# A new table of operations for an attention and MLP kernel: what stands where in each engine's queue

## The chip, the cores and the metric

The kernel runs on one core of a Trainium2 chip. The metric is device time in microseconds (us) of one execution; the time of a version is the median of several runs. A profile shows one execution, instruction by instruction, on the engines TensorE (PE, with its weight loads as PEld), VectorE (DVE), ScalarE (ACT), GpSimd (POOL) and the queue of SyncE that issues DMAs (SP).

## The reference

For 2048 tokens of width 512 the kernel computes an attention layer, gated by an MLP, and a residual:

```python
def _A_ref(x, wqkv, wo):                     # 32 heads of 16, window of 8 keys, 2 apart
    qkv = (x @ wqkv).reshape(B, S, 3, H, Dh) ...
    idx = pos[:, None] - (jnp.arange(8) * 2)[None, :]
    logits = einsum("bhsd,bhswd->bhsw", q, k[idx]) * scale      # idx < 0: -1e9
    o = einsum("bhsw,bhswd->bhsd", softmax(logits), v[idx])
    return o.reshape(B, S, D) @ wo
def _B_ref(x, w1, b1, w2, b2):
    return gelu(layernorm(x) @ w1 + b1) @ w2 + b2               # 512 -> 1376 -> 512
xn = layernorm(A_x)
return A_x + _A_ref(xn, ...) * silu(_B_ref(xn, ...))
```

## The kernel before

The tokens are split into two halves by parity (c = 0, 1), since the window goes in steps of 2, and each half into 8 tiles of 128 tokens. Every matrix is held as a high and a low half of 16 bits, and a product is three matmuls (high-high, high-low, low-high), summed in PSUM.

The work is a list of 1262 operations, each with one engine, a few instructions, and the data that it reads and writes:

- Loading and normalising the tokens, L659 to L773: statistics, y = (x - mean) / deviation on ACT (L744), DVE (L751) or POOL (L748), a transpose on PE (L766) and the split of the result (L770, L773). Two tiles are projected directly in 32-bit floats (L700).
- Projections q, k, v (PE, L864; 12 matmuls of 384 columns for a tile and a quarter of the heads), brought out of PSUM by ACT (L882) or DVE (L878) into a buffer U.
- Eight units of attention, one for each half and quarter of the heads, nearly all on DVE: products of q and shifted keys (L930), their sums (L933), softmax (L953 to L962), products with the values (L988, in the last unit L1026) and their sums (L983; on POOL L998 and L1008). The result is split into halves (ACT L971, DVE L973) and transposed by a DMA (L976).
- The MLP: first layer on PE (L1141), gelu and high half on ACT (L1154, L1157), low half on DVE (L1159), second layer on PE (L1184, with a last narrow block at L1172 and L1175), silu on ACT (L1195, L1200).
- The output layer: for the first half of the tokens L1054 on PE, the gate on DVE (L1068), the residual (L1045) and the store (L1048); for the second half L1086, L1118, the residual on DVE (L1125) or POOL (L1122), and the stores (L1127). In the second half the matmuls of three quarters of the heads come first and those of the last quarter, whose transposed attention is the last to come, later into the same PSUM tile. The last tile is computed and stored in two parts of 256 columns.
- 24 filler matmuls without a use (L1303).

What sets the order: `Plan.issue` takes the operations one after another from the table `ORDER` (it holds each operation's number once) and emits their instructions. Each engine runs its instructions in this order and waits, at each, for the data or the buffer that it needs; nothing behind it on the same engine passes. The table also decides which buffer an operation gets: rings of a few tiles (`ps` 3 and `z` 4 in PSUM, `pl` 1, `prod` 3, `h` 3, `f` 7) hand out the tile that was given back first, in the order of the table:

```python
            for b in o.bufs:
                b.left -= 1
                b.end = max(b.end, end)
                if not b.left:
                    b.ring.free[b.slot] = len(order) if ORDER else b.end
```

Of the kernel before, what the change touches and what calls it, by code (L numbers as in the profile page):

```python
# [70 lines left out]
BEFORE_W1 = (0, 1, 4, 5)  # L71

ORDER = (
# [62 lines left out]
)  # L136


class Buf:


    def __init__(self, ring):
        self.ring, self.slot, self.left, self.end = ring, None, 0, 0.0
# [1381 lines left out]
```

## Time and profile before

| what | value |
|---|---|
| runs | 417.12, 417.95, 418.23 us; median 417.95 |
| profiled execution | 418.01 us |
| its span, first to last instruction | 416.2 us |
| granted TensorE clock, mean | 0.996 |
| busy: PE, DVE, ACT, POOL | 97%, 92%, 55%, 32% of the span |

A busy share says how much of the span an engine had work in hand. In the rows below a timeline row gives the start in us, the duration in us, engine, line, operation and tiles; "x12" means twelve instructions in a row, and a bracket at the end gives the idle time ahead and what ended it. A row of a stretch gives its bounds, its length, the busy time of PE, PEld, DVE, ACT and POOL in it, the granted clock, the share of the DMA engines and the GB/s. A wait row gives the waiting operation, the one that it waited for, the total in us, how often, and the longest.

### The profile page before, as it was taken

The page shows a single profiled execution, that of the slowest core. Times are in us where ns is not written, and L with a number is a line of the kernel's source. Part 1 is how long each engine was busy: PE and PEld are TensorE (multiplying, and loading weights), DVE is VectorE, ACT ScalarE, POOL GpSimd, SP SyncE. Part 2 cuts the span into 40 slices and gives each one's busy share as a digit, 9 for nine tenths or more (in the row PEclk, how much of TensorE's full clock was granted, in tenths as well). Part 3 has the DMA queues.
Part 4 walks back from the last instruction along what each step waited for, and adds up shares of the span by engine and source line. Part 5 has one row for each costly group of instructions (what it writes and reads, how often), then busy time and mean ns, then how long its engine had stood idle before and what let it go on. Part 6 is the DMA issues. An engine that isn't in the chain of part 4 may idle for free.

```text
span 416.2 us, 5499 instructions
## 1 busy us (share of the span) xinstructions
PE 404.3 (97%) x2035; PEld 199.9 (48%) x2035; DVE 383.4 (92%) x386; ACT 227.8 (55%) x374; POOL 134.3 (32%) x134
## 2 busy tenths in 40 slices
PE   8799999999999999999999999999999999999992
PEld 4465544444444455445544544444445444444441
DVE  3998999999999999999889989999999999989974
ACT  3799988886878656553566254124414375253220
POOL 3833000062943334143414434252423304420031
PEclk9999999999999999999999999999999999999998
DMA  8946709250009560544170129002261346018236
GB/s 280 397 95 194 265 1 262 75 175 2 2 16 191 116 178 0 113 102 71 45 178 14 43 65 249 4 25 64 94 205 57 84 111 186 18 28 230 79 77 227
DMA packets 52627, 48.04 MB, mean 115 GB/s; under 512 B 37066, under 2 KB 37510, under 8 KB 52088
## 3 DMA queue, kind: packets, MB, share of 16 engines
q1 hardware_dynamic: 52600, 47.69, 41.5%
q8 instruction: 16, 0.26, 0.3%
q14 instruction: 11, 0.09, 0.1%
HBM read 24.40 MB, written 7.34 MB: 76 GB/s over the span
## 4 chain that ended last, share of the span: by engine, by line
PE 93%; DVE 3%; ACT 1%; DMA 1%; issue 0%; DVEq 0%
PE ps L864 28%; PE ps L1141 25%; PE z L1184 24%; PE ps L1054 5%; PE ps L1086 2%; PE z L1086 2%; PE z L1172 2%; PE pl L864 1%; PE pl L700 1%; DMA U<-in_A_xt_dram 1%; PE pl L1086 1%; PE z L1175 1%; DVE lw L651 1%; DVE L L933 0%; DVE bn L659 0%
## 5 line engine op out<-in xcount | busy, mean ns | idle before, releaser
L864 PE MATMUL ps<-wq,yT 128*128 128x384 f16 (+1 forms) x708 | 128.5, 337 | 0.2 <-ACT yT L770 0.2
L1184 PE MATMUL z<-w,h 128*128 128x512 f16 x480 | 111.2, 379 | 0.0
L1141 PE MATMUL ps<-yT,w 128*128 128x512 f16 x480 | 109.5, 379 | 0.7 <-DVE h L1159 0.7
L864 PEld LDWEIGHTS <-yT 128*128 128x128 f16 x744 | 72.5, 98 | 58.2 <-ACT yT L770 0.5
L930 DVE TENSOR_TENSOR prod<-U 128x2048 f32<-128x2048 f32 x32 | 73.0, 2287 | 1.3 <-DMA U<-U 0.2
L1141 PEld LDWEIGHTS <-w 128*128 128x128 f16 x480 | 46.6, 98 | 56.4 <-issue 1.7
L933 DVE TENSOR_REDUCE L<-prod 128x128 f32<-128x2048 f32 x32 | 72.9, 2281 | 0.4
L1184 PEld LDWEIGHTS <-h 128*128 128x128 f16 x480 | 46.6, 98 | 55.0 <-issue 0.2
L998 POOL TENSOR_TENSOR prod<-prod,prod 128x2048 f32<-128x2048 f32 x7 | 40.3, 5757 | 88.2 <-DVE prod L988 88.2
L882 ACT ACTIVATE U<-ps,cs 128x384 f32<-128x384 f32 x54 | 30.9, 578 | 64.1 <-PE ps L864 60.7
L988 DVE TENSOR_TENSOR prod<-pl,U 128x2048 f32<-128x2048 f32 x28 | 63.6, 2284 | 0.4
L1154 ACT ACTIVATE ps<-ps,b1T,hsc 128x512 f32<-128x512 f32 x40 | 29.6, 748 | 30.6 <-PE ps L1141 29.6
L1157 ACT ACTIVATE h<-ps,hsc 128x512 f16<-128x512 f32 x40 | 27.3, 685 | 22.2 <-PE z L1184 17.6
L1007 POOL COPY gate<-prod 1x1 f32<-1x1 f32 x21 | 5.2, 246 | 98.8 <-DVE prod L930 98.8
L1008 POOL TENSOR_TENSOR prod<-prod 128x1024 f32<-128x1024 f32 x14 | 32.9, 2350 | 0.0
L1159 DVE SCALAR_TENSOR_TENSOR h<-ps,hsc,h 128x512 f16<-128x512 f32 x40 | 29.7, 744 | 3.2 <-ACT h L1157 3.1
L1054 PE MATMUL ps<-wo,oT 128*128 128x512 f16 x96 | 21.7, 379 | 0.0
L983 DVE TENSOR_TENSOR prod<-prod,prod 128x2048 f32<-128x2048 f32 x9 | 20.6, 2284 | 0.1
L1008 POOL TENSOR_TENSOR prod<-prod,prod 128x1024 f32<-128x1024 f32 x7 | 16.4, 2341 | 0.0
L1122 POOL TENSOR_TENSOR U<-U,f 128x512 f32<-128x512 f32 x3 | 4.6, 1542 | 34.8 <-DVE U L1118 34.8
L1086 PEld LDWEIGHTS <-oT 128*128 128x128 f16 x108 | 10.4, 98 | 10.2 <-issue 0.5
L1054 PEld LDWEIGHTS <-oT 128*128 128x128 f16 x96 | 9.4, 98 | 11.1
(201 smaller groups left out, 410.7 us busy)
## 6 DMA issues: line engine op xcount, KB each, us to landing
f<-in_A_x_dram SPq DMA_DIRECT2D x31, 256.0 KB
U<-U SPq DMA_DIRECT2D x16, 392.0 KB
gd<-f SPq DMA_DIRECT2D x12, 256.0 KB
prod<-in_A_x_dram SPq DMA_DIRECT2D x8, 256.0 KB
oT<-in_B_w_dram SPq DMA_DIRECT2D x2, 1024.0 KB
yT<-in_B_w_dram SPq DMA_DIRECT2D x2, 1024.0 KB
f<-gd SPq DMA_DIRECT2D x8, 256.0 KB
out_dram<-f SPq DMA_DIRECT2D x8, 256.0 KB
```

The lines of the kernel that those rows point to most:

```text
L864: nc.tensor.matmul(b.t[:, 0:wide], y[:, s, k, o:o + P], wq[hb][:, t, k], start=(n == 0), stop=(n == 11))
L882: act(384, lambda i=i, b=b: nc.scalar.activation(U3[:, i:i + 31:15, :], b.t[:, 0:384].rearrange("p (t e) -> p t e", t=3), AF.Identity, sca ...
L930: dve(2048, lambda p2=p2, g=g: nc.vector.tensor_tensor(p2(), q, slots(Ut, KH, 2 * g), op=ALU.mult), qk + [("kh", ub, 0), ("kh", ub, 1), (" ...
L933: dve(2048, lambda pr=pr, g=g: nc.vector.tensor_reduce(L3()[:, 2 * g:2 * g + 2], pr.t.rearrange("p (r f d) -> p r f d", r=2, d=DH), AX.X, ...
L988: dve(2048, lambda: nc.vector.tensor_tensor(pr.t.rearrange("p (r f d) -> p r f d", r=2, d=DH), A3()[:, 2 * g:2 * g + 2].rearrange("p r (f ...
L998: pool(4.75, lambda: nc.gpsimd.tensor_tensor(acc.t, acc.t, p1.t, op=ALU.add), [acc, p1], [acc])
L1008: nc.gpsimd.tensor_tensor(x.t[:, 0:1024], x.t[:, 0:1024], y(), op=ALU.add)
L1054: nc.tensor.matmul(b.t, oT[:, hb, i // 4, s, i % 4], wo[:, t, hb], start=(hb == 0 and n == 0), stop=(hb == last and n == 2))
L1086: nc.tensor.matmul(b.t[:, cols], oT[:, hb, i // 4, s, i % 4], wo[:, t, hb, cols], start=(start and hb == 0 and n == 0), stop=(stop and hb ...
L1141: nc.tensor.matmul(b.t[0:M], w1[:, s, f * 512 + k * M:f * 512 + (k + 1) * M], yT[ch][:, t, k], start=(n == 0), stop=(n == 11))
L1159: dve(512, lambda: nc.vector.scalar_tensor_tensor(lo()[0:M], b.t[0:M], hsc[0:M, 2:3], hi()[0:M], op0=ALU.mult, op1=ALU.subtract), [b, hk], ...
L1184: nc.tensor.matmul(z.t, hl[s][:, t * P:(t + 1) * P], w2[:, w, f], start=(f == 0 and n == 0), stop=False)
```

## The change

The table `ORDER` is replaced by another one over the same 1262 operations; no other line changes. It is one line shorter, so every line behind it has a number lower by one: L1127 is L1126 in the changed kernel, and so on. The first lines of the table, cut:

```diff
 ORDER = (
-    0, 1, 19, 2, 115, 130, 132, 129, 128, 114, 117, 120, 133, 124, 131, 121, 116, 111, 119, 20, 113, 21, 112,
+    0, 1, 19, 2, 112, 125, 113, 130, 121, 132, 124, 122, 111, 117, 131, 115, 114, 126, 120, 32, 33, 3, 4, 5, 6,
...
```

**The end of the program.** On SP, before, from the last transpose of the attention (oT) on; U holds the results of the second half, f_108 the last one of the first half, and x is loaded for the residual:

```order
L976 DMA_TRANSPOSE oT<-o_112 128x8x128
L1108 DMA f_105<-in_A_x_dram 128x512
L1127 DMA out_dram<-U_93 128x256
L1127 DMA out_dram<-U_93 128x512 x6
L1048 DMA out_dram<-f_108 128x512
L1127 DMA out_dram<-U_93 128x512
L1127 DMA out_dram<-U_93 128x256
```

and now, from the store of the first half's last result (here f_109) on:

```order
L1047 DMA out_dram<-f_109 128x512
L975 DMA_TRANSPOSE oT<-o_112 128x8x128
L1107 DMA f_108<-in_A_x_dram 128x512
L1107 DMA f_109<-in_A_x_dram 128x512
L1126 DMA out_dram<-U_93 128x512
L1126 DMA out_dram<-U_93 128x256
L1126 DMA out_dram<-U_93 128x512 x6
L1126 DMA out_dram<-U_93 128x256
```

The store of f has moved from third last to ahead of the transpose, and a store of 512 columns ahead of the first one of 256.

On DVE the last instructions before are these (`pl`, `ps` and `z` are PSUM tiles that PE fills, L1118 scales and gates them into U, L1125 adds x):

```order
L1118 SCALAR_TENSOR_TENSOR U_93<-z_148,osc,U_93 128x512
L1125 TENSOR_TENSOR U_93<-U_93,f_107 128x512
L1118 SCALAR_TENSOR_TENSOR U_93<-z_150,osc,U_93 128x256
L1125 TENSOR_TENSOR U_93<-U_93 128x256
L1118 SCALAR_TENSOR_TENSOR U_93<-z_147,osc,U_93 128x512
L1118 SCALAR_TENSOR_TENSOR U_93<-ps_143,osc,U_93 128x256
L1118 SCALAR_TENSOR_TENSOR U_93<-z_149,osc,U_93 128x512
L1125 TENSOR_TENSOR U_93<-U_93 128x256
L1125 TENSOR_TENSOR U_93<-U_93,f_109 128x512
```

and now:

```order
L1117 SCALAR_TENSOR_TENSOR U_93<-z_150,osc,U_93 128x256
L1124 TENSOR_TENSOR U_93<-U_93 128x256
L1117 SCALAR_TENSOR_TENSOR U_93<-ps_143,osc,U_93 128x512
L1117 SCALAR_TENSOR_TENSOR U_93<-z_147,osc,U_93 128x512
L1117 SCALAR_TENSOR_TENSOR U_93<-z_148,osc,U_93 128x512
L1124 TENSOR_TENSOR U_93<-U_93,f_109 128x512
L1117 SCALAR_TENSOR_TENSOR U_93<-z_149,osc,U_93 128x512
L1124 TENSOR_TENSOR U_93<-U_93,f_103 128x512
L1117 SCALAR_TENSOR_TENSOR U_93<-ps_144,osc,U_93 128x256
L1124 TENSOR_TENSOR U_93<-U_93 128x256
```

The last result of 512 columns (z_149) now comes whole ahead of the last one of 256. PE's order has moved with it: z_150 (256 columns, with 3 matmuls of the last quarter of the heads), then z_147 and z_148 (3 each), z_149 (9 and 3) and, last, ps_144 (12 of 256 columns); before, the group of 9 for z_149 stood some 16 us ahead of the end, and its 3 matmuls were the last.

**The start.** On PE before, from a transpose of a normalised tile to the first projection (prod_101 holds the tile, first the identity; L513 sums squares):

```order
L766 MATMUL z_150<-first,prod_101 128x128 x4
L700 MATMUL z_148<-prod_100,U_94 128x384 x2
L513 LDWEIGHTS fours
L513 MATMUL ps_145<-s_126,fours 128x1
L1303 LDWEIGHTS fours
L1303 MATMUL z_147<-first,fours 128x256
L766 MATMUL z_150<-first,prod_101 128x128 x4
L700 MATMUL z_148<-prod_100,U_94 128x384
L864 LDWEIGHTS yT_89
L864 MATMUL ps_143<-wq_82,yT_89 128x384
```

and now:

```order
L1302 LDWEIGHTS fours
L1302 MATMUL z_147<-first,fours 128x256
L699 MATMUL z_148<-prod_100,U_94 128x384
L765 MATMUL z_149<-first,prod_101 128x128 x4
L512 LDWEIGHTS fours
L512 MATMUL ps_145<-s_127,fours 128x1
L699 MATMUL z_148<-prod_100,U_94 128x384
L863 LDWEIGHTS yT_89
L863 MATMUL ps_143<-wq_82,yT_89 128x384
```

Another tile (into z_149, normalised by DVE at L750) is transposed ahead of the first projection than before (into z_150, normalised by ACT at L744). Five fillers that stood between the first L700s have left that place, where three L699 now stand in a row; three fillers stand behind the first projection matmuls, where one stood.

**The attention of the second to last unit and the output of the first half.** On DVE before:

```order
L930 TENSOR_TENSOR prod_102<-U_93 128x2048
L827 SCALAR_TENSOR_TENSOR hrem<-hl_98,hsc,f_106 128x4x32
L933 TENSOR_REDUCE L_110<-prod_102 128x2x64
L930 TENSOR_TENSOR prod_102<-U_93 128x2048
L933 TENSOR_REDUCE L_110<-prod_102 128x2x64
L947 MEMSET L_110 1x8
L953 TENSOR_REDUCE mx_116<-L_110 128x64
L954 TENSOR_TENSOR L_110<-L_110,mx_116 128x512
L1068 SCALAR_TENSOR_TENSOR f_105<-ps_145,osc,f_105 128x512
L1045 TENSOR_TENSOR f_105<-f_105,f_104 128x512
```

and now:

```order
L929 TENSOR_TENSOR prod_100<-U_93 128x2048
L1067 SCALAR_TENSOR_TENSOR f_107<-ps_143,osc,f_107 128x512
L932 TENSOR_REDUCE L_110<-prod_100 128x2x64
L929 TENSOR_TENSOR prod_100<-U_93 128x2048
L932 TENSOR_REDUCE L_110<-prod_100 128x2x64
L1067 SCALAR_TENSOR_TENSOR f_109<-ps_144,osc,f_109 128x512
L946 MEMSET L_110 1x8
L952 TENSOR_REDUCE mx_116<-L_110 128x64
L953 TENSOR_TENSOR L_110<-L_110,mx_116 128x512
```

The gate of that output tile (L1068 into f_105, now L1067 into f_107) has moved from behind the softmax's first steps to right behind the third product; its matmuls on PE moved ahead of one group of 12 at L1054 and two of 12 at L864.

121 rows, old and new, of the table ORDER are left out of this document.

## The prediction

> **What bounds the kernel now.** I read the page's busy shares first, then the stretches before, during and after the dense matmul work, then PE's own waits, and last the timeline of the two ends.
>
> ```profile
> span 416.2 us, 5499 instructions
> PE 404.3 (97%) x2035; PEld 199.9 (48%) x2035; DVE 383.4 (92%) x386; ACT 227.8 (55%) x374; POOL 134.3 (32%) x134
> 0.00:18.51 18.51, 14.88 (x62) 8.91 (x63) 11.62 (x39) 9.94 (x17) 9.74 (x18) 1.00 0.92 337
> 18.51:408.88 390.37, 389.44 (x1975) 190.99 (x1973) 370.14 (x345) 217.82 (x358) 124.15 (x117) 1.00 0.39 102
> 408.88:416.20 7.32, 0.00 (x0) 0.00 (x0) 1.68 (x3) 0.00 (x0) 0.45 (x1) 0.77 0.80 294
> PE z L766 <- ACT prod L744: 1.9, 1, 1.9
> PE ps L1141 <- DVE h L1159: 0.7, 1, 0.7
> PE ps L864 <- ACT yT L770: 0.2, 1, 0.2
> ```
>
> From the first projection matmul (18.51) to the last matmul (408.88) PE is busy 389.44 of 390.37 us. The two lower wait lines are all that it loses there, 0.9 us. A reordering keeps every matmul, so it can win this 0.9 us, something of the 18.5 us ahead, and something of the 7.3 us behind; it can lose without limit in the middle. The 7.3 us is the odd one: DVE works for 1.68 us of it and PE not at all.
>
> ```profile
> 406.75 1.47 PE L1086 MATMUL ps<-wo,oT 128*128 128x256 f16 x12
> 408.06 0.81 PE L1086 MATMUL z<-wo,oT 128*128 128x512 f16 x3
> 408.91 0.75 DVE L1118 SCALAR_TENSOR_TENSOR U<-z,osc,U 128x512 f32<-128x512 f32 x1 [0.16 <-PE z L1086]
> 409.58 0.41 DVE L1125 TENSOR_TENSOR U<-U 128x256 f32<-128x256 f32 x1
> 409.91 0.68 DVE L1125 TENSOR_TENSOR U<-U,f 128x512 f32<-128x512 f32 x1
> 407.35 4.09 SPq L1127 DMA_DIRECT2D out_dram<-U  x7
> 411.50 0.45 SPq L1048 DMA_DIRECT2D out_dram<-f  x1
> 411.99 1.16 SPq L1127 DMA_DIRECT2D out_dram<-U  x2
> 408.00:409.00 1.00, 0.87 (x6) 0.24 (x3) 0.57 (x2) 0.00 (x0) 0.93 (x1) 1.00 0.72 246
> 409.00:410.00 1.00, 0.00 (x0) 0.00 (x0) 1.00 (x3) 0.00 (x0) 0.33 (x1) 1.00 1.03 385
> 413.00:414.00 1.00, 0.00 (x0) 0.00 (x0) 0.00 (x0) 0.00 (x0) 0.00 (x0) 0.50 1.04 387
> 414.00:415.00 1.00, 0.00 (x0) 0.00 (x0) 0.00 (x0) 0.00 (x0) 0.00 (x0) 0.50 0.73 256
> ```
>
> The last arithmetic ends at 409.91 + 0.68 = 410.59, yet SP is still issuing stores until 411.99 + 1.16 = 413.15. All ten stores start at 407.35, because the first of them in SP's order (the 256-column one) is ready only then; from there SP issues about one each 0.58 us (4.09 / 7) and the DMA engines run full (385 to 387 GB/s, share 1.03) until about 414.7. So the end is a backlog of stores: SP's order sets it, not arithmetic.
>
> **The change part by part.**
>
> *The stores.* Call X the end of the last matmul, 408.87 before. The rows of the changed SP order put the L1047 store ahead of the last transpose and one full store ahead of the 256-column one; the last 256-column store stands behind six others. Nothing is removed: it is the time at which each may start that moves. The store of f (L1048) needs only this row, 14 us ahead of its old issue:
>
> ```profile
> 396.49 0.69 DVE L1045 TENSOR_TENSOR f<-f,f 128x512 f32<-128x512 f32 x1
> 401.96 3.33 POOL L1122 TENSOR_TENSOR U<-U,f 128x512 f32<-128x512 f32 x2 [32.06 <-DVE U L1118]
> 405.00 0.75 DVE L1118 SCALAR_TENSOR_TENSOR U<-z,osc,U 128x512 f32<-128x512 f32 x1 [0.83 <-PE z L1086]
> 406.39 0.48 DVE L1118 SCALAR_TENSOR_TENSOR U<-z,osc,U 128x256 f32<-128x256 f32 x1
> 406.90 0.42 DVE L1125 TENSOR_TENSOR U<-U 128x256 f32<-128x256 f32 x1
> ```
>
> The new first full store needs the first POOL addition, at about 401.9 + 1.7 = 403.6 even unchanged. The 256-column one needs the rows of 0.48 and 0.42 us. On PE its matmuls now stand ahead of 3 + 3 matmuls of 512 columns, a whole group of 12, and the closing 12 of 256. At 0.216 us a matmul of 512 columns (0.65 for 3) and 1.31 for the closing dozen (408.06 - 406.75), that is 0.65 + 0.65 + 2.59 + 1.31 = 5.2 us ahead of X; plus 0.9 on DVE, ready at X - 4.3. So SP has eight stores over the 5.4 us from X - 4.3 to X + 1.1, and eight at 0.58 are 4.6: it keeps up, if no single one comes late.
>
> The last store then waits for arithmetic alone. The last 512-column result is whole at X - 1.31; its two DVE steps (0.75 + 0.68, started 0.04 later) end at X + 0.16; the last 256 columns take 0.48 + 0.41 behind them: X + 1.05, against X + 1.72 before. Issue from X + 1.08. From issue to the first bytes: SP's first store begins at 407.35, and the window 408 to 409 moved 246 of the 385 GB/s of a full one, so bytes flow from about 408.36: 1.0 us. 128 KB at 385 GB/s: 0.34. From the last bytes (414 + 256 / 387 = 414.66) to the span's end, 416.2: 1.5. Sum: X + 1.08 + 1.0 + 0.34 + 1.5 = X + 3.9, against X + 7.33 before, with an empty queue. If the queue stays as full as now, the old distance from the end of the last issue to the span's end, 416.2 - 413.15 = 3.05, stands: X + 1.08 + 0.65 + 3.05 = X + 4.8. I take X + 3.9, as SP and the DMA engines have caught up by then, and keep X + 4.8 for the range. This term is worth -3.4 us, at least -2.5.
>
> *The start.*
>
> ```profile
> 6.18 1.65 PE L700 MATMUL pl<-prod,U 128*128 128x384 f32 x2 [0.35 <-DVE U L693]
> 8.05 1.49 PE L700 MATMUL pl<-prod,U 128*128 128x384 f32 x2
> 10.07 0.89 PE L700 MATMUL pl<-prod,U 128*128 128x384 f32 x2
> 17.27 0.54 DVE L751 TENSOR_SCALAR prod<-prod,mv,rb 128x512 f32<-128x512 f32 x1
> 17.37 0.66 PE L766 MATMUL z<-first,prod 128*128 128x128 f32 x4 [1.89 <-ACT prod L744]
> 17.86 0.81 PE L700 MATMUL z<-prod,U 128*128 128x384 f32 x2
> 18.51 0.81 PE L864 MATMUL ps<-wq,yT 128*128 128x384 f16 x4
> 49.85 0.27 PE L1303 MATMUL z<-first,fours 128*128 128x256 bf16 x1
> ```
>
> PE's last wait before the dense part is for a normalised tile. Now another tile, from the 0.54 us DVE instruction, stands there. That one moves ahead of an L773 (0.68) and a small one (0.15) on DVE, so it ends 0.6 to 0.8 earlier, at 17.1; transposes (0.5) and the last L699 (0.65) follow, and the first L863 starts near 18.4: no real change from 18.51. Behind it three filler matmuls stand in the dense part where one stood (49.85): two more of 0.1 us. The first accumulators are released in another sequence by DVE; I found two places where PE could wait 0.2 to 0.3 us. Together +0.3, from -0.3 to +1.3.
>
> *The middle.* The moved groups cancel in the sum, and only waits count. The 0.7 us wait at L1141 should go: its matmuls now take an accumulator whose last reader is ACT, not the late L1159 on DVE. Going through PE's new order with row times against the producers' places on DVE and ACT, I find no place where a producer stands clearly behind its user; the covers are mostly 1 us and more, the smallest 0.2 to 0.5 (a matmul group near 58 us and one near 289). As some covers will be missed, I count -0.4, from -0.7 to +1.5.
>
> X becomes 408.87 + 0.3 - 0.4 = 408.8; the span 408.8 + 3.9 = 412.7. The profiled execution took 418.01, 1.81 more than its span; so 414.5. It lies 0.06 above the median, 417.95, so I leave 414.5 as the median too.
>
> **The rivals.**
>
> *1. DVE comes late to the last attention (slower).* In the changed DVE order an L1067 stands right behind the third L929, ahead of these:
>
> ```profile
> 321.04 2.28 DVE L933 TENSOR_REDUCE L<-prod 128x128 f32<-128x2048 f32 x1
> 329.00 0.69 DVE L954 TENSOR_TENSOR L<-L,mx 128x512 f32<-128x512 f32 x1
> 329.95 0.75 DVE L1068 SCALAR_TENSOR_TENSOR f<-ps,osc,f 128x512 f32<-128x512 f32 x1 [0.26 <-PE ps L1054]
> 324.51 5.34 PE L1054 MATMUL ps<-wo,oT 128*128 128x512 f16 x24
> 398.55 1.24 SPq L976 DMA_TRANSPOSE oT<-o  x1
> 400.50:401.50 1.00, 1.00 (x6) 0.47 (x5) 1.00 (x3) 0.00 (x0) 0.00 (x0) 1.00 0.61 108
> 401.50:402.50 1.00, 1.00 (x7) 0.47 (x5) 1.00 (x3) 0.00 (x0) 0.54 (x1) 1.00 0.00 0
> ```
>
> DVE would reach it about 329.69 - 321.04 = 8.6 us earlier, less 0.35 for a small step that now precedes: 321.7. Its matmuls move ahead of one L1054 group (2.59) and two L864 groups (1.95 each), and end at 329.85 - 6.5 = 323.4. So DVE stands about 1.5 us there, and everything behind it in its queue, the last attention above all. That attention ends in the transpose at 398.55, which has landed by 401.5 (DMA share 0.61, then 0.00). PE's first use of it is now 5.5 us ahead of X, 403.3: 1.8 us of cover. So 1.5 us costs nothing; with D us of delay in all, PE stands D - 1.8, and the time is 414.5 + D - 1.8. It is slower than now by over 0.3% from D = 6.5; at 8 it is 420.7. For it speaks DVE's 92%; against it that DVE is idle for 20 us of the dense stretch (390.37 - 370.14), some of which this order may use. Chance 0.10 for a slower result, by this or by waits of the middle that add up to as much.
>
> *2. The start loses.* Before 10.07 a pair of L700 takes 1.5 us, from there 0.8 to 0.9: PE runs at half rate until 10 us. The changed order takes fillers out of that stretch, though three L699 in a row fill it. If full rate came some 3 us later, the matmuls from 10.1 to 13.5 would take twice as long, at most +3.4, partly hidden by DVE's own chain: +1.5 to +3, so 416 to 417.5. The Trainium skill, "TensorE: Matmul & The Clock Gate", Part 1, says that PE's full clock is granted after about 3.4 us of sustained activity, in windows that run free of the kernel; by that rule fewer fillers could defer it by one window, and two runs of one kernel could differ. Rows agree on the half rate, not on what releases it. Chance 0.10.
>
> *3. The tail is not given back.* One store that comes late, such as POOL's last addition, holds those behind it in SP's queue, and the ends move little: -1 us at best, 417 to 418. The ten stores are 2.36 MB, 6.2 us at 385 GB/s, so this holds if they still start together. Against it stands the new order of SP. Chance 0.10.
>
> **How the numbers follow.** My forecast has 0.70: 414.5, by its bounds from 408.87 - 0.7 + 3.9 + 1.8 = 413.9 to about 416.7 (X + 4.8 and +1.3 at the start). The range takes in rival 2: 413.5 to 417.5. A measurement of this kernel can tell about 0.3%, 1.25 us, from no change. Faster than 416.7: the forecast and 0.6 of rival 2, 0.76. Within: the rest of rival 2 and most of rival 3, 0.12. Slower: rival 1 and a little of rival 3, 0.12.
>
> **What would show it.** Right: SP's last issue ends within 2 us of the last matmul, the stretch behind X is about 4 us, PE's waits from 18.5 on stay under 1 us, and the last matmul ends within 1 us of 408.8. Wrong: waits of L1183 or L1140 for DVE's L1158 of 2 us each, a wait of L1085 for the last transpose, a first L863 after 20, or a last store that still ends over 4 us behind X.

## The result, and the profile after

The changed kernel took 413.88 us (median of 5 runs, 413.27 to 415.19) against 417.95 (5 runs, 416.79 to 419.23): the ratio is 0.9906, with a 95% interval of 0.9879 to 0.9932. Forecast were 414.5 us, 413.5 to 417.5, and faster. The profiled execution took 413.27 us, 1.77 more than its span.

The first two lines of its page:

```profile
span 411.5 us, 5502 instructions
PE 402.0 (98%) x2035; PEld 199.2 (48%) x2035; DVE 383.0 (93%) x386; ACT 226.0 (55%) x373; POOL 132.7 (32%) x134
```

Its stretches, cut at the first projection matmul and at the last matmul, as before (bounds, length, busy time of PE, PEld, DVE, ACT and POOL, granted clock, DMA share, GB/s):

```profile
0.00:17.16 17.16, 12.63 (x60) 7.99 (x61) 11.31 (x39) 9.52 (x18) 9.72 (x18) 1.00 0.91 342
17.16:407.57 390.41, 389.33 (x1977) 191.18 (x1975) 370.55 (x348) 216.50 (x356) 123.01 (x117) 1.00 0.41 106
407.57:411.50 3.93, 0.00 (x1) 0.00 (x0) 1.10 (x3) 0.00 (x0) 0.00 (x0) 0.97 0.51 185
```

The span is 4.7 us shorter: 3.39 of it lie behind the last matmul (7.32 before, 3.93 now), 1.35 ahead of the first projection matmul (18.51, now 17.16), and nothing between (390.37, now 390.41). PE's waits from 10 us on in this execution:

```profile
PE z L517 <- ACT w L503: 1.1, 1, 1.1
PE z L699 <- DVE U L692: 1.1, 1, 1.1
PE z L765 <- DVE prod L750: 0.8, 1, 0.8
```

The wait at L1140 (0.7 at L1141 before) is gone. The one at L517, at 52.0 us, is new; the other two rows are of the start. The end in the timeline:

```profile
395.76 0.34 SPq L1047 DMA_DIRECT2D out_dram<-f  x1
396.73 1.24 SPq L975 DMA_TRANSPOSE oT<-o  x1
399.35 9.72 SPq L1126 DMA_DIRECT2D out_dram<-U  x9
400.90 5.36 PE L1085 MATMUL z<-wo,oT 128*128 128x256 f16 x30
406.10 1.47 PE L1085 MATMUL ps<-wo,oT 128*128 128x256 f16 x12
407.76 0.48 DVE L1117 SCALAR_TENSOR_TENSOR U<-ps,osc,U 128x256 f32<-128x256 f32 x1
408.28 0.43 DVE L1124 TENSOR_TENSOR U<-U 128x256 f32<-128x256 f32 x1
```

The store of f is issued at 395.76; the nine others are spread over 399.35 to 409.07, where all ten stood between 407.35 and 413.15 before. The last arithmetic ends at 408.71, the last issue 0.36 behind it.

### The profile page after: what moved, and what is told of

The parts are those of the page before. It is cut to its first block, busy times and chain, and to the rows that moved or that the text cites. A ratio compares the mean times of both kernels' runs of the same rounds, so it can differ in the third digit from the quotient of the medians.

```text
span 411.5 us, 5502 instructions
## 1 busy us (share of the span) xinstructions
PE 402.0 (98%) x2035; PEld 199.2 (48%) x2035; DVE 383.0 (93%) x386; ACT 226.0 (55%) x373; POOL 132.7 (32%) x134
## 4 chain that ended last, share of the span: by engine, by line
PE 91%; DMA 4%; DVE 2%; SPq 2%; ACT 1%; issue 0%; DVEq 0%
PE ps L863 27%; PE z L1183 25%; PE ps L1140 24%; PE ps L1053 5%; DMA yT<-in_B_w_dram 2%; PE z L1085 2%; PE ps L1085 2%; PE z L1171 2%; PE pl L863 1%; DMA prod<-in_A_x_dram 1%; PE pl L1085 1%; PE z L1174 1%; DVE bn L658 1%; ACT w L503 0%; SPq L1267 0%; SPq L895 0%
## 5 line engine op out<-in xcount | busy, mean ns | idle before, releaser
L1140 PE MATMUL ps<-yT,w 128*128 128x512 f16 x480 | 109.8, 379 | 0.0
L1140 PEld LDWEIGHTS <-w 128*128 128x128 f16 x480 | 46.6, 98 | 56.9 <-issue 2.0
L997 POOL TENSOR_TENSOR prod<-prod,prod 128x2048 f32<-128x2048 f32 x7 | 38.3, 5476 | 75.3 <-DVE prod L987 75.3
L970 ACT ACTIVATE o<-prod,osc 128x1024 f16<-128x1024 f32 (+1 forms) x9 | 9.4, 1049 | 14.7 <-DVE prod L982 14.0
L1085 PEld LDWEIGHTS <-oT 128*128 128x128 f16 x108 | 10.5, 98 | 10.4 <-issue 0.2
```

The costliest lines, as they stand in the source:

```text
L997: pool(4.75, lambda: nc.gpsimd.tensor_tensor(acc.t, acc.t, p1.t, op=ALU.add), [acc, p1], [acc])
L1085: nc.tensor.matmul(b.t[:, cols], oT[:, hb, i // 4, s, i % 4], wo[:, t, hb, cols], start=(start and hb == 0 and n == 0), stop=(stop and hb ...
L1140: nc.tensor.matmul(b.t[0:M], w1[:, s, f * 512 + k * M:f * 512 + (k + 1) * M], yT[ch][:, t, k], start=(n == 0), stop=(n == 11))
```

## The experiments

All kernels but e11 and e12 hold the same instructions; only the order differs. In seven of them (e1 to e4 and e6 to e8) the table is cut: the numbers of one table up to a place, then those that are left in the sequence of the other. "Before" is the kernel before on the same chip.

| run | median us | before | ratio, 95% interval |
|---|---|---|---|
| e1_tail | 416.67 | 417.79 | 0.9974 (0.9962 to 0.9986) |
| e2_no_tail | 417.89 | 417.79 | 1.0008 (0.9996 to 1.0021) |
| e3_start | 418.61 | 417.79 | 1.0028 (1.0014 to 1.0041) |
| e4_start_tail | 417.81 | 417.79 | 1.0001 (0.9989 to 1.0014) |
| e5_stores_only | 414.93 | 417.76 | 0.9934 (0.9918 to 0.9950) |
| e6_cut_345 | 415.60 | 417.76 | 0.9949 (0.9931 to 0.9967) |
| e7_cut_220 | 414.04 | 417.76 | 0.9909 (0.9890 to 0.9929) |
| e8_old_start | 414.45 | 417.76 | 0.9919 (0.9901 to 0.9938) |
| e9_again | 413.62 | 417.78 | 0.9908 (0.9892 to 0.9924) |
| e10_l518_later | 414.17 | 417.78 | 0.9921 (0.9908 to 0.9935) |
| e11_fill | 413.68 | 417.78 | 0.9914 (0.9897 to 0.9931) |
| e12_dve_late | 418.08 | 417.78 | 1.0017 (0.9999 to 1.0036) |

### The end alone, and everything but the end

```diff
 ..., 1157, 1158, 1161, 1162, 1163, 1164, 925, 1159, 1253, 1248,
-    1243, 1204, 1212, 1200, 1203, 1205, 1165, 1202, 1209, 1166, 1229, 1234, 1224, 1219, 1211, 1210, 1225, 1220,
...
-    1240, 1258, 1249, 1259, 1250, 1260, 1251, 1238, 1241, 1257, 1232, 1222, 1242, 1247, 1252, 1237, 926, 1227, 1261,
+    1200, 1202, 1203, 1165, 1205, 1204, 1166, 1211, 1209, 1229, 1224, 1234, 1210, 1219, 1213, 926, 1167, 1230,
...
+    1227, 1220, 1212, 1249, 1258, 1240, 1245, 1246, 1221, 1222, 1247, 1241, 1250, 1251, 1259, 1260, 1242, 1252, 1261,
```

This is e1_tail (the kernel before with the last 52 operations in the new sequence); e2_no_tail is the reverse edit of the changed table.

> The first 1210 operations stand in the order of before, the last 52 in the order of the changed table. Theory (the parts add up, and the tail is the store backlog): from the last matmul to the end of the span 3.9 us instead of 7.3, the first projection matmul stays at about 18.5, the matmul stretch at 390.4; time 417.95 - 3.4 = 414.5. Rival 1 (the tail gains only because the changed middle brings its inputs earlier): PE waits in the last 15 us, or the stores still bunch; behind the last matmul 5 us or more, 415.5 to 418. Rival 2 (the stores are not the cause; what gained is start and middle): 417.5 to 418.

> The mirror image: the first 1210 operations in the changed order, the last ones in the order of before, so that the store of the 256 columns is first in SP's queue and the store of f third last. Theory: behind the last matmul about 7.3 us again; 413.88 + 3.4 = 417.3. Rival 1 (the tail needs the changed middle, and the middle carries some of the gain): 414.5 to 416.5. Rival 2 (start and middle made the gain): 413.9 to 414.5.

The stretch behind e2's last matmul:

```profile
409.35:416.70 7.35, 0.01 (x1) 0.00 (x0) 1.69 (x3) 0.00 (x0) 0.46 (x1) 0.85 0.80 294
```

It is 7.35 us again, and the gain is gone: the new start and middle by themselves are worth nothing that these runs can tell (a wait of 0.8 us at L1086, made by the cut, stands against them). But the new end by itself is worth only 1.1 us, not 3.4. Two rows of e1's profile say why, first its waits, then the stretch behind its last matmul:

```profile
PE z L1086 <- ACT U L1195: 1.4, 1, 1.4
```

```profile
411.02:415.60 4.58, 0.00 (x0) 0.00 (x0) 1.81 (x4) 0.00 (x0) 0.00 (x0) 0.78 0.55 200
```

PE stands 1.4 us for a tile z that ACT's silu (L1195) has still to empty, since in the order of before the last MLP tile is finished later than the new end supposes (its last L1175 ends at 394.6, right ahead of the wait; in the changed kernel at 392.5); and the end is 4.6 instead of 3.9 us. My theory that the parts add up fell here. Rival 1 had the time and the wait, though it counted on an end of 5 us or more.

### The start alone, and start with end

```diff
-ORDER: the 1262 numbers of before
+e3: the first 97 of the changed table, the rest in the sequence of before
+e4: the same, and from number 1211 on the sequence of the changed table
```

> The first 97 operations (up to about 19 us) in the changed order, the rest in the order of before. Theory (the start gains by its order): the first projection matmul at 17.2 us instead of 18.5, full TensorE rate from about 6 us (two 32-bit matmuls of 384 columns in 0.8 us there, not 1.5 to 1.65), tail 7.3; 417.95 - 0.7 to - 1.35 = 416.6 to 417.3. Rival (when full rate comes is a matter of the single execution, not of the order): half rate until 10 us in this profile too, or the first projection matmul at 18 or later; 417.9. Rival 2 (the start loses where it meets the middle of before): over 418.5.

> Changed order for the first 97 operations and for those behind the 1210th; between them the order of before. Theory (the middle is worth nothing): 413.9, as the changed kernel; the 0.7 us wait of PE at L1141 for DVE's L1159 is back, and the matmul stretch is as long as in both. Rival 1 (the middle won 0.7 by that wait): 414.6. Rival 2 (the middle cost something that the other parts hide): 413.2 or less, and this would be the best version.

e3 is slower by 0.8 us, although its first projection matmul starts at 17.45: right behind it PE waits for a normalised tile, which the order of before brings later. That is rival 2, a seam.

```profile
PE ps L864 <- ACT yT L770: 1.2, 1, 1.2
```

e4 has that wait (0.7), the one at L1141 (0.7), the one at L1086 for L1195 (1.4) and an end of 4.6 us: 2.8 + 0.7 = 3.5 us, of which 1.1 is set off by the changed kernel's own wait at L517. That is 2.4 of the 3.9 us by which it stands above the changed kernel; for the other 1.5 I have no row. So these four pieces don't show what a part is worth, as each of the cuts makes waits of its own. Whoever reads e4 as "the middle is worth 3.9 us" is misled; e2 has nearly the whole new middle and wins nothing.

### Only SP's queue

This edit needs no cut, as the rows of the four compute engines stay as they were in before. The difference on SP:

```
+L1048 DMA out_dram<-f_108 128x512
 L976 DMA_TRANSPOSE oT<-o_112 128x8x128
 L1108 DMA f_105<-in_A_x_dram 128x512
+L1127 DMA out_dram<-U_93 128x512 x5
 L1127 DMA out_dram<-U_93 128x256
-L1127 DMA out_dram<-U_93 128x512 x6
-L1048 DMA out_dram<-f_108 128x512
 L1127 DMA out_dram<-U_93 128x512
 L1127 DMA out_dram<-U_93 128x256
+L1127 DMA out_dram<-U_93 128x512
```

> The kernel before, with only SP's queue changed: the store of f ahead of the last transpose, the nine stores of the second half sorted by the time at which their data were whole in the trace of before (402.5 to 410.6 us). PE, DVE, ACT and POOL keep their rows. Theory (the end was a backlog that SP's order made): last arithmetic at 410.6 as before, the last issue right behind it, 1.0 + 0.34 x 2 + 1.5 us to the end of the span: 413.8 instead of 416.2, so 417.8 - 2.4 = 415.4. Rival 1 (without PE's new order the stores bunch all the same, or the early store of f holds the transpose up): 417 to 418. Rival 2 (the backlog is all of it, also what the changed kernel wins by its arithmetic): 414.0 to 414.5.

414.93: 2.8 us, two thirds of the whole gain, by ten entries in one queue. The stretches of its profile, then the end of its timeline:

```profile
17.50:407.86 390.36, 389.45 (x1975) 190.99 (x1973) 370.24 (x345) 217.71 (x358) 124.21 (x117) 1.00 0.40 106
407.86:412.60 4.74, 0.00 (x0) 0.00 (x0) 1.69 (x3) 0.00 (x0) 0.47 (x1) 0.75 0.39 139
```

```profile
396.56 0.43 SPq L1048 DMA_DIRECT2D out_dram<-f  x1
397.54 1.29 SPq L976 DMA_TRANSPOSE oT<-o  x1
401.88 8.07 SPq L1127 DMA_DIRECT2D out_dram<-U  x9
408.90 0.69 DVE L1125 TENSOR_TENSOR U<-U,f 128x512 f32<-128x512 f32 x1
```

The matmul stretch is that of before (390.36 against 390.37). Behind it DVE works for 1.69 us as before (1.68), yet the span ends 4.74 us behind the last matmul and not 7.32: the last issue is over at 409.95, 0.36 behind the last arithmetic (409.59). That the end was a backlog of SP's order is shown by this run alone. The time lies between the theory (415.4) and rival 2 (414.0 to 414.5); which of the two moves gives how much, the early store of f or the full stores ahead of the one of 256 columns, is not separated. Of the other 0.8 us of the end (4.74 to 3.93), 0.59 come from PE's and DVE's new order there: the last arithmetic ends 1.14 us behind the last matmul in the changed kernel, 1.73 here. The other 0.22 lie between the end of the last issue and the end of the span (2.65 here, 2.43 there); the last store has 512 columns here and 256 there.

### How far back the new end reaches

```diff
-ORDER: the 1262 numbers of before
+e6: the first 1080 of before (to 345 us), the rest in the sequence of the changed table
+e7: the first 780 of before (to 220 us), the rest in the sequence of the changed table
```

> The order of before for the first 1080 operations (to about 345 us), the changed order from there. In e1_tail, cut at 392 us, PE waited 1.4 us at L1086 for ACT's L1195, as the tile z had still to be emptied by the silu of an MLP tile that the changed order finishes some us earlier. Theory (the end of the changed table needs its own order from about 380 us on, and nothing earlier): that wait is gone, 3.9 to 4.2 us behind the last matmul, 417.8 - 3.2 = 414.6. Rival 1 (the changed order from before 345 us is needed as well): 415.5 to 416.7. Rival 2 (the end is worth no more than in e1_tail): 416.7.

> The order of before for the first 780 operations (to about 220 us), the changed order from there. Theory: as e6_cut_345, 414.6; the order between 220 and 345 us is worth nothing. Rival (it prepares the end): better than e6_cut_345 by 0.7 or more.

In both the wait of 1.4 us is gone. e7 is as fast as the changed kernel, e6 is not, and their intervals don't quite meet: 415.6 and 414.04, so the theory fell for e6 (rival 1 had its time) and the rival for e7 was right. As e7 has the order of before up to 220 us, it keeps the gain without the new start and without the first half of the new middle. The difference that the timelines show is at the end, where POOL and DVE both add two tiles of SBUF. First e6, then e7:

```profile
406.36 2.49 POOL L1122 TENSOR_TENSOR U<-U,f 128x512 f32<-128x512 f32 x2 [4.86 <-DVE U L1118]
407.63 1.77 DVE L1125 TENSOR_TENSOR U<-U,f 128x512 f32<-128x512 f32 x1
411.22 0.42 DVE L1125 TENSOR_TENSOR U<-U 128x256 f32<-128x256 f32 x1
```

```profile
406.26 3.04 POOL L1122 TENSOR_TENSOR U<-U,f 128x512 f32<-128x512 f32 x2 [4.91 <-issue]
407.47 0.69 DVE L1125 TENSOR_TENSOR U<-U,f 128x512 f32<-128x512 f32 x1
410.31 0.42 DVE L1125 TENSOR_TENSOR U<-U 128x256 f32<-128x256 f32 x1
```

In e6 POOL's second addition goes first and DVE's takes 1.77 us instead of 0.69; in e7 (and in the changed kernel, 3.04 too) DVE's goes first and POOL's pair takes longer. POOL's next result is needed late, DVE's stands ahead of the last gates: e6's last arithmetic ends at 411.64, 1.88 us behind its last matmul (409.76); e7's at 410.73, 1.13 behind (409.60). e1 and e4, with the order of before up to 392 us, have the same 1.77; e8 to e11 have the 0.69 and 3.04 of e7. The Trainium skill, "SBUF — State Buffer", section "SBUF: two separate sides", says that a port pair which both engines need is an exclusive lock: whoever starts first holds it for the whole instruction. The rows agree. Less than a tenth of a microsecond decides who that is, and 0.7 us hang on it. The other 0.8 us between the two medians are not explained by a row that I found; the two profiled executions differ by 0.91 us only (416.26 and 415.35).

### The start, once more

```diff
-ORDER: the 1262 numbers of the changed table
+e8: the first 97 of before, the rest in the sequence of the changed table
+e9: the changed table, unedited
```

> The order of before for the first 97 operations (to about 19 us), the changed order from there. Six profiles show that the rate of the early matmuls differs between executions of one order, so the profiled 17.16 against 18.51 us says little of the order. Theory (the new start costs some tenths, since PE waits more in it and so runs more often at half rate): 413.1 to 413.6, below the 413.88 of the changed kernel. Rival 1 (the new start is what its profile showed, worth 0.7 to 1.35): 414.6 to 415.2. Rival 2 (a seam as in e3_start, PE waiting about 1 us for ACT's L770): over 414.6 with that wait in the profile.

> The changed table once more, unedited, on the chip that the three other kernels of this round run on. Theory: 413.9; behind the last matmul 3.9 us; PE waits 1.1 us at L518 for ACT's L504. How fast the start is, 17.2 to 19.5 at the first projection matmul, differs by execution.

e8 has a wait at its seam (1.1 us at L766) and can't be told from the changed kernel; it is not below it, as its theory had it (413.1 to 413.6). e9 says more of the start: the same kernel, another execution, and its stretches are these:

```profile
0.00:19.81 19.81, 15.12 (x59) 9.42 (x60) 11.94 (x39) 10.69 (x20) 10.59 (x18) 0.83 0.91 343
19.81:409.77 389.96, 389.34 (x1977) 191.25 (x1975) 370.59 (x348) 215.56 (x354) 121.85 (x116) 1.00 0.40 104
409.77:413.70 3.93, 0.00 (x1) 0.00 (x0) 1.10 (x3) 0.00 (x0) 0.00 (x0) 1.00 0.51 185
```

The first projection matmul at 19.81 instead of 17.16, the end the same to the hundredth. The granted clock is 0.83 in the mean of its start; here it is, us by us:

```profile
11.00:12.00 1.00, 0.02 (x1) 0.00 (x0) 0.97 (x4) 1.00 (x4) 1.00 (x1) 0.65 1.06 408
12.00:13.00 1.00, 0.92 (x2) 0.62 (x3) 0.93 (x5) 0.92 (x2) 0.33 (x1) 0.50 1.08 435
...
17.00:18.00 1.00, 1.00 (x6) 0.73 (x5) 0.92 (x3) 0.97 (x3) 1.00 (x2) 0.50 1.14 423
18.00:19.00 1.00, 1.00 (x7) 0.67 (x6) 0.00 (x0) 1.00 (x2) 1.00 (x1) 0.93 1.04 420
```

From about 11.3 to 18.1 PE's clock is halved, for twice 3.4 us. Of the seven profiles that have the new start, two have a halved clock from about 11 us on for 3.4 us (e2, e10), two for twice that (e4, e9) and three not at all; their first projection matmuls stand at 17.16, 17.45, 18.19, 18.33, 18.54, 19.50 and 19.81, 18.33 in the middle. What differs ahead of it is the wait of PE for the second load of the tokens (L681; L682 in the others): 1.4 to 1.8 us in those four, 1.0 us or less in the three others. Here are the three microseconds from 8 on in the changed kernel's first profile, in e9, and in e5 with the old start:

```profile
8.00:11.00 3.00, 1.48 (x11) 1.06 (x9) 2.23 (x10) 1.79 (x4) 2.07 (x2) 1.00 1.05 401
8.00:11.00 3.00, 1.22 (x11) 0.97 (x8) 2.23 (x10) 1.04 (x2) 1.32 (x2) 1.00 1.05 403
8.00:11.00 3.00, 2.19 (x12) 1.19 (x10) 2.10 (x10) 2.27 (x5) 1.89 (x2) 1.00 1.04 392
```

PE is busy 1.22 to 1.40 us of them in the four with a halved clock, 1.48 and 1.63 in two of the others (in the third, e12, its matmuls still take twice as long until 10 us, and so they fill the stretch). That the idleness brings the fall fits these rows; no edit here shows it alone. The old start varies as well: 17.50, 17.63, 17.80, 17.89, 18.19 and 18.51 in six profiles. It has more work at this place (1.93 to 2.19 us in five, and the half rate until 10 in the sixth) and no fall at 11 us; but in three profiles the clock is halved for 3.4 us from about 18 on, behind the wait of 1.9 us at L766 that all six have. So either start has a place at which the clock may fall. Six and seven profiles don't tell which order is shorter, and the 1.35 us that the two starts differ by in the profiles above can't be put down to the order.

### A wait taken out of the middle

On PE, six matmuls of L1141 pass ahead of the step that waited:

```
+L1141 LDWEIGHTS w_86
+L1141 MATMUL ps_143<-yT_89,w_86 128x512
...
 L518 LDWEIGHTS fours
 L518 MATMUL z_147<-s_130,fours 128x6
-L1141 LDWEIGHTS w_86
-L1141 MATMUL ps_143<-yT_89,w_86 128x512
...
```

> The changed table with one step moved: the matmul at L518 that sums the squares of w2 stands six matmuls of L1141 later on PE. In the changed kernel PE waited 1.08 us there for ACT's L504, which ends at 52.0 in both profiles since its weights land at 50.0. Theory (that wait is the loss of the changed order's middle): the wait goes, the stretch to the last matmul is 1.1 shorter, 413.9 - 1.1 = 412.8. Rival 1 (the step is passed on: DVE and ACT get the scale later and PE waits for them at L1184 or L1141): 413.9. Rival 2 (slower, as DVE's L930 behind it starts late): over 414.3.

The wait at L518 went and nothing was won (414.17 against 413.62 for e9 on the same chip). PE's waits in e10 hold the one that took its place, 5 us later:

```profile
PE ps L1141 <- DVE h L1159: 0.9, 1, 0.9
```

That is rival 1's mechanism: what stands behind L518, the scale of w2, comes later too, and ACT and DVE pass the delay on. Its producer still waits for the weights:

```profile
51.27 1.91 ACT L504 ACTIVATE w<-yT 128x2048 bf16<-128x2048 f32 x1 [1.44 <-DMA yT<-in_B_w_dram]
```

In the changed kernel's first profile the weights let it start at 49.97. My expectation took that moment as fixed at 50.0; it differs by execution (52.17 in e9). Six matmuls later for this one step did not get round the wait; other places were not tried.

### Matmuls without a use where PE idles

```diff
-    pl.add("pe", 0.2, lambda b=b: nc.tensor.matmul(b.t[:, 0:2 * P], fours, mean1.bitcast(BF16), start=True,
-                                                   stop=True), [], [b], prio=1e9)
+    pl.add("pe", 0.2, lambda b=b, k={18: 4, 19: 9, 13: 8}.get(n, 1): [nc.tensor.matmul(
+        b.t[:, 0:2 * P], fours, mean1.bitcast(BF16), start=True, stop=True) for _ in range(k)], [], [b], prio=1e9)
```

> As e10_l518_later, and three of the filler steps (L1303) stand in PE's three idle places of the start (9, 10.3 and 15 us) and issue 4, 9 and 8 matmuls without a use there. In two of four profiles of the new start the 32-bit matmuls from 11.7 to 15.2 us and on ran at half rate, and in those two PE's waits before them had been longest. Theory (idle time in the start lets PE's rate drop): two matmuls of 384 columns take 0.8 to 0.9 us all through the start, the first projection matmul at 17.2 to 17.5 in nearly every execution, and the median 0.5 to 0.9 below e10_l518_later. Rival 1 (the rate does not depend on it): the same as e10_l518_later. Rival 2 (the fillers delay what stands behind them): 0.5 to 1.5 above.

In e11 the three fillers also stand elsewhere in the table, and the step at L518 stands as in e10. Pairs of 384 columns take 0.9 us or less all through the start of its profile, as the theory has it, but the first projection matmul stands at 17.76, not at 17.2 to 17.5. PE is busy 2.00 of the three microseconds from 8 on, and the clock does not fall there. It is steadier over the six runs: the mean granted clock is 0.998 to 1.000, where five of the eleven runs of the changed kernel (with e9's) have 0.992 to 0.995. The time isn't better: 413.68, with an interval that holds e9's and e10's ratios. Six runs don't separate 0.5 us here, so whether the fillers pay stays open.

### The price of a late DVE

```diff
-    dve(2048, lambda ...: nc.vector.tensor_tensor(..., win, op=ALU.mult), ...)
+    dve(2048, lambda ...: [nc.vector.tensor_tensor(..., win, op=ALU.mult) for _ in range(1 + h)], ...)
```

> The changed table, and both products of L1026 in the second half of the last attention are issued twice on DVE, so that the last transpose is issued 4.57 us later (2 x 2.28); the results are the same. The prediction gave this place 1.8 us of cover and D - 1.8 beyond it: 413.9 + 2.8 = 416.7, with PE waiting 2.8 us at L1086. Rival 1 (the cover is larger, since the transpose lands well ahead of PE's first use): 413.9 + 1.5 to 2.2. Rival 2 (no cover, as DVE is late for the last gates as well): 413.9 + 4 to 4.6.

It costs 4.5 us (418.08 against 413.62), near rival 2, but not by rival 2's mechanism: the last arithmetic still ends 1.1 us behind the last matmul. Two of PE's waits, then the end of the timeline, then the stretches around the wait:

```profile
PE z L1086 <- DMA oT<-o: 2.4, 1, 2.4
PE pl L1086 <- DVE prod L1026: 0.9, 1, 0.9
```

```profile
401.94 1.24 SPq L976 DMA_TRANSPOSE oT<-o  x1
402.55 1.15 PE L1086 MATMUL z<-wo,oT 128*128 128x256 f16 x9
406.07 5.99 PE L1086 MATMUL z<-wo,oT 128*128 128x256 f16 x21 [2.38 <-DMA oT<-o]
```

```profile
402.00:403.70 1.70, 1.69 (x13) 0.97 (x10) 1.70 (x3) 0.24 (x1) 1.08 (x1) 1.00 0.81 184
403.70:406.07 2.37, 0.00 (x1) 0.01 (x1) 1.35 (x3) 0.00 (x0) 0.18 (x1) 0.97 1.06 138
406.07:408.00 1.93, 1.93 (x7) 0.92 (x8) 0.97 (x3) 0.00 (x0) 0.00 (x0) 0.50 0.83 313
408.00:410.00 2.00, 2.00 (x8) 0.81 (x7) 1.77 (x3) 0.00 (x0) 1.27 (x2) 0.66 0.55 197
```

PE waits 2.4 us for the transpose and 0.9 us for a tile that the doubled L1026 reads longer; that is 3.3, near the 2.8 of the theory. The rest is the clock: behind the 2.4 us of idleness it is halved until about 409.3, and 21 matmuls take 5.99 us that took some 4.2 in the changed kernel (5.36 for 30, less 1.15 for the same first nine). 3.3 + 1.8 is 5.1, somewhat over the measured 4.5. The account holds for this execution, one of the longer ones (419.03 us; the twelve runs go from 416.51 to 420.62). Two of the twelve have a granted clock of 1.000 and took 417.03 and 417.44, so not every run can have the halved stretch, and what it adds to the median is open.

## Why the prediction held, step by step

*The end.* Forecast: X + 3.9 behind the last matmul, measured X + 3.93. Inside it, the last arithmetic was to end at X + 1.05 and ends at X + 1.14; SP's last issue was to keep up and ends at X + 1.50. "SP's order sets it, not arithmetic" is shown by e5, where only SP's order moves, the matmul stretch stays at 390.36 and the end shrinks by 2.58.

*The middle.* Forecast -0.4, measured +0.04 in the first profile of the changed kernel (390.41) and -0.41 in the second, e9 (389.96). The wait at L1141 went as foreseen. What I missed is the wait at L517, 1.08 and 0.62 us: of the covers that I called small I named a place near 58 us, and the short one was at 52, where a matmul had moved ahead of 1.3 us of others while its producer, L503, waits for weights until 49.97. In e9 PE comes to that place 2.7 us later, by its start, and the weights 2.2 us later (52.17), so the wait is shorter. The two more fillers in the stretch, 0.2 us, had been counted with the start.

*The start.* Forecast +0.3, at most 0.3 below; the profile showed -1.35. The size was wrong for this execution, and the step behind it too: I took the order's work alone to set the start, where the clock and the landing of a load, which differ by execution, move it by up to 2.65 us (e9). The rival that named the clock was right in this, also that two runs of one kernel would differ. Its own step, that fewer fillers put off the full rate, is not seen: from about 6 us on six matmuls of L699 take 2.20 us in six of the seven profiles of the new start, and only e12 has the half rate until 10 (4.16 us for the six), as before has. What was lost instead is the rate at 11 us; and since the old start can lose it at 18, no loss against before shows in the times.

*Rival 1, DVE late.* DVE waits at L1067 as foreseen, and PE never waits for it:

```profile
322.16 0.75 DVE L1067 SCALAR_TENSOR_TENSOR f<-ps,osc,f 128x512 f32<-128x512 f32 x1 [2.46 <-PE ps L1053]
```

The 2.46 us stand against the 1.5 worked out, where the prediction's own 323.4 - 321.7 gives 1.7. e12 shows the price: the transpose is of use to PE 4.1 us behind its issue (401.94 to 406.07), in the changed kernel at 400.9, and PE's nine matmuls ahead of the first use end at about 402.0. The cover is 1.1 us, not the 1.8 of the text, which took the transpose as landed 2.95 us behind its issue because the DMA engines were idle then. Beyond the cover the price can be more than D less the cover, by a half-rate stretch.

*Rival 3, the end not given back.* Nothing of it is seen in the changed kernel; e1, e4 and e6, with ends of 4.6 us, show that it could have been in part.

*The sum.* Forecast X = 408.8 and a span of 412.7; the two profiles have 407.57 and 409.77, and spans of 411.5 and 413.7. So the end came out as worked out, while X was missed by 1.2 one way and 1.0 the other; that the medians lie within 0.9 us of the forecast is owed to the end, and to chance in the start. Two of the four signs of being right were not met in the first profile: a wait behind 18.5 reached 1.08 us, and the last matmul ended 1.2 us from 408.8. 0.3 - 0.4 - 3.4 = -3.5 stands against -4.07 and -4.16 of the medians; of these e5 accounts for 2.8, and the rest of the end, read from profiles, for about 0.6 to 0.8. What is left, 0.5 us, lies within the intervals. The bounds of the forecast each leave a term out: with the -0.3 of the start the lower is 413.6, and with the -0.4 of the middle the upper is 416.4.

## What to carry to other kernels

Where transfers end a program, look when each one's data is whole and in which sequence one queue issues them: ten entries sorted by readiness gave two thirds of this gain without touching a compute engine. A gap between the last arithmetic and the last issue is the sign, 2.6 us before and 0.4 now. Judge a reordered table whole or by edits that leave all other queues as they are; pieces cut out of it can bring waits of their own (e1 to e4), and a profile of one execution does not tell an early start from a fast clock.

## What the runs showed of the hardware

The granted clock falls to 0.50 without a long idle stretch. In e12 2.4 us of idleness were enough, with PE busy 1.14 of the 3.42 us ahead of the fall; in e9 it was 1.34 of 3.40 us, in two waits of 1.8 and 1.1 us. The halved stretches last 3.4 us or twice that. The Trainium skill, "TensorE: Matmul & The Clock Gate", Part 1, says that half rate comes back after at least one idle window of about 3.4 us and that the window runs free of the kernel; the length agrees, but here 3.4 us in which PE worked a third to two fifths of the time were enough, and the measurement decides. That the window runs free of the kernel is shown by no run here, as the executions differ in PE's waits too. In e12's profile a wait of 2.4 us on PE cost 4.2 in this way. In the first 10 us of before and of e12 the clock's column reads 1.00 although the matmuls of L700 take twice as long as later (1.5 us a pair against 0.8); there only the durations show the half rate.

An addition of two SBUF tiles on DVE that meets one on POOL took 1.77 us instead of 0.69, or lengthened POOL's pair from 2.49 to 3.04, by who came first.
